# Adding the last quarter of each first product in PSUM, onto a copy that ScalarE makes

## The chip, the cores and the metric

The kernel runs on one core of a Trainium2 chip. The metric is the device time of one launch in microseconds (us), as a median over runs. Five engines work side by side, each through its own queue in program order: TensorE (PE, matrix products; its weight loads are shown apart as PEld), VectorE (DVE), ScalarE (ACT), GpSimd (POOL) and SyncE (SP, which issues most DMAs).

## The reference, cut to what matters

```python
# attention: B, H, S, D = 4, 8, 768, 64, in blocks of 64 tokens, with a decay lam per head
for b in range(nb):
    intra = einsum('bhij,bhjd->bhid', einsum('bhic,bhjc->bhij', qb, kb) * Dmask, vb)
    inter = einsum('bhid,bhde->bhie', qb * lam_pow, kv_state)
    out[:, :, sl] = intra + inter
    kv_state = lam_block * kv_state + einsum('bhsd,bhse->bhde', kb * rev_pow, vb)
x = out.transpose(0, 2, 1, 3).reshape(3072, 512)
# four experts (branches), all of them for every token
p = domain_probs / (domain_probs.sum(-1, keepdims=True) + 1e-09)
for e in range(4):
    h = np.maximum(x @ w1[e], 0.0)           # 3072x512 @ 512x1024
    out += p[:, e:e + 1] * (h @ w2[e])       # 3072x1024 @ 1024x512
```

All is float32. The two products with w1 and w2 are nearly all of the arithmetic.

## The kernel before, in words

The 3072 tokens go in three groups of 1024, and a *unit* is one expert on one group: twelve units, numbered 0 to 11. For each unit the *first product* is relu(x @ w1) and the *second product* is the gated product with w2. While unit `at` has its second product, unit `at + 1` has its first one: TensorE goes back and forth between the two. Attention of the later groups is put between them in the first units.

Both products use Strassen's scheme in Winograd's form: seven products M1 to M7 in place of eight, with sums before and after. The first product uses it twice, so one unit's first product consists of seven outer products `m` (in the order `SEQ` = M1, M5, M6, M2, M7, M3, M4), and each of those has seven inner ones `i` (in the order `INNER` = M1, M7, M6, M4, M5, M2, M3). An outer product is called a *product* below, and an inner one a *piece*. One piece is two fp32 matmuls of 128x128 by 128x256 into the two halves of one PSUM bank; the profile shows each matmul as two records, so a piece is four.

`first_product` (matmuls at L1053) works with two PSUM banks, g1 and g3. Pieces are summed in PSUM as far as Winograd's sums allow, and the bank is read in between:

- g1: M1 begins; it is read for quarter "11"; M6 is added, read for "21"; M5 is added, read for "22"; M3 is added, read for "12".
- g3: M7 begins, read for "22"; M4 is added, read for "21"; then a fresh bank is begun by M2, read for "11".

A read is an addition by VectorE (`tt`, L117) into the quarter's SBUF tile `new[at]`, 128x512, or a copy by ScalarE (L1061) where nothing is there yet to add to. The next matmul that writes the same bank has to wait for the read. Products that finish one quarter of relu(x @ w1) (`OUT` = M2, M3, M4) are passed through a relu by ScalarE in place (L1065). From unit 5 on (`NEST` = 5) the gate is multiplied in at once, by GpSimd in place (`gated`, L117 on POOL), because these units have a nested second product. `finished` and `later` add M5's, M6's and M7's sums afterwards as background steps; there ScalarE copies one operand into a PSUM bank (`bring`, "up" at L985, 128x512 from SBUF to PSUM) and VectorE adds from it.

The second product has two forms. In units 0 to 4 it is *flat* (`second_product`, L1107): each of its seven steps has four parts of four matmuls, eight records each. In units 5 to 11 it is *nested* (`nested_product`, L1406): each step has seven pieces b0 to b6, of two matmuls, four records, each; VectorE adds each to `sums` after it is made.

So there are 77 first products beside a second one: 35 beside a flat one (of units 1 to 5) and 42 beside a nested one (of units 6 to 11). The order of TensorE's work within each pair is written out by hand, in eight *slots* x = 0 to 7. `a` is the list of the first product's pieces and `b` that of the second product's:

```python
elif nested:
    order = [b[0:2], a[0:2], b[2:4], a[2:4], b[4:6], a[4:6], b[6:8], a[6:8]]
else:
    order = [b[0:1], a[0:2], b[1:2], a[2:4], b[2:3], a[4:6], b[3:5], a[6:8]]
```

The last entry of `a` is `finished`, and b[7] (nested) or b[4] (flat) is a step that issues nothing on TensorE. Between the slots a background step may be taken (`rest`, `take`): sums for later operands (`hT`, `xs`, `sums<-sums,jp`) on VectorE, with their copies by ScalarE (`hp` at L905). Weights and other work for GpSimd are let out by counters (`pump`, `fits`) that the planner keeps of each engine's supposed load.

Of the kernel before, what the change touches and what calls it, by code (L numbers as in the profile page):

```python
# [11 lines left out]
AF = mybir.ActivationFunctionType  # L12
ALU = mybir.AluOpType
# [8 lines left out]
def kernel(  # L22
# [30 lines left out]
    nc = tc.nc  # L53

    B, H, S, D = q.shape
    E, DM, F = moe_w1.shape
    NTOK, DOUT = out.shape
    P = nc.NUM_PARTITIONS
# [9 lines left out]
    W = 512  # L68
# [20 lines left out]
    def bank(tag, name):  # L89
        return ps.tile([P, W], FP32, name=name, tag=tag)  # L90
# [25 lines left out]
    def tt(eng, o, a, b, op):  # L116
        eng.tensor_tensor(out=o, in0=a, in1=b, op=op)  # L117
        if eng is nc.gpsimd:
            busy[0] = max(busy[0], now[0]) + math.prod(o.shape[1:]) / (640 if spare else 480)
        else:  # L120
            vector(math.prod(o.shape[1:]), PSUM in (a.space, b.space))

    def vector(n, psum):
        filled[0] = max(filled[0], now[0] + psum / 2) + 0.09 + n * (0.31 if psum else 0.8 if spare else 0.49) / 512
# [14 lines left out]
    unit_of = {u: x for x, u in enumerate(units)}  # L139
    NEST = 2 * E - 3  # L140
# [52 lines left out]
    def store(f):  # L193
        queue.append((busy[0] + (8 if spare else 2), f))
# [35 lines left out]
    def inner(eng, what, to, blk, ops, at):  # L230

        b = {n: blk[:, i, j * 256:(j + 1) * 256] for n, (i, j) in at.items()}
        s = stage.tile([P, 4, 256], FP32, name="ops", tag="st")
        for i, (name, x, y, op) in enumerate(ops):
            b[name] = s[:, SLOT[name]]
            tt(eng, b[name], b[x], b[y], op)
        pieces = [(to[:, 1:5], s[:])]
        if A_OF[what[2]][0] == "S":
            pieces += [(to[:, 0], blk[:, 0, 0:256]), (to[:, 5:7], blk[:, 1].rearrange("p (a f) -> p a f", a=2))]
        store(lambda: ([send(out=x, in_=y) for x, y in pieces], made.add(what)))  # L240
# [81 lines left out]
    INNER = ("M1", "M7", "M6", "M4", "M5", "M2", "M3")  # L322
# [194 lines left out]
    for r in range(2):  # L517
        for ac in range(NHP):
            h = 4 * r + ac
            nc.vector.tensor_tensor_scan(  # L520
                out=s_decay[:, r, ac], data0=lam_bc[:, h:h + 1].to_broadcast([P, BL]), data1=blk_ident,
# [10 lines left out]
    for ac in range(NHP):  # L532
        nc.vector.tensor_tensor_scan(
            out=q_decay[:, ac], data0=lam_q[:, ac:ac + 1].to_broadcast([P, BL]), data1=zeros[:, 0:BL],
# [22 lines left out]
    gate_bc = decay[:]  # L557
# [40 lines left out]
    def after(slots, f):  # L598

        f = functools.partial(f)  # L600
        f.at = now[0] + slots
        return f
# [10 lines left out]
    def rest(n=1, force=False):  # L613
        for _ in range(n):
            take(background, force)
# [262 lines left out]
    outer = {e: {n: {} for n in ("B11", "B12", "B21", "B22", "T1", "T2", "T3", "T4")} for e in range(NEST, len(units))}  # L878
    within = {}

    def gated(e, i, j, at, t):

        def step():
            n = j * 4 + (int(at[1]) - 1) * 2
            x = t[:].rearrange("p (c t) -> p c t", c=2)
            by = gate_bc[:, n:n + 2].rearrange("p n t -> p (n t)").unsqueeze(1).to_broadcast([P, 2, 256])
            tt(nc.gpsimd, x, x, by, ALU.mult)
            outer[e][f"B{i + 1}{j + 1}"][at] = t

        aside.append(after(2, step))  # L890
# [84 lines left out]
    OUT = {"M2": (0, 0), "M3": (0, 1), "M4": (1, 0)}  # L975

    def finished(g, e, m, blocks, new):

        def later(to, a, b, order, relu=False):
            there = dict(a)  # L980

            def bring(at):

                there[at] = bank("s" + "01"[order.index(at) % 2], "up")
                nc.scalar.copy(out=there[at][:], in_=a[at][:])  # L985

            def step(at):
                x = there[at]
                if unit_of[g, e] >= NEST and at != order[-1]:
                    bring(order[order.index(at) + 1])  # L990
                o = to[at] if at in to else small("m" + at)
                tt(nc.vector, o[:], x[:], b[at][:], ALU.add)
                if relu:
                    nc.scalar.activation(out=o[:], in_=o[:], func=AF.Relu)
                    if unit_of[g, e] >= NEST:
                        gated(unit_of[g, e], 1, 1, at, o)
                to[at] = o
                blocks["left"] -= 1

            blocks["left"] = 4  # L1000
            if unit_of[g, e] >= NEST:
                background.append(lambda: bring(order[0]))
            background.extend(lambda at=at: step(at) for at in order)

        def keep(c, i, j):
            if unit_of[g, e] >= NEST:
                outer_sums(unit_of[g, e], *{(0, 1): (("T1",), ("T3", "T2")), (1, 0): (("T4",),)}.get((i, j), ()))
                return
            hid[g, e, i, j] = {"A11": c["11"], "A12": c["21"], "A22": c["22"], "A21": c["12"]}
            operands((g, e, i, j))  # L1010

        if m == "M6":
            blocks["U2"], blocks["U4"] = new, {}
            later(blocks["U4"], new, blocks["M5"], ("11", "22", "21", "12"))
        elif m == "M7":
            blocks["U3"] = new
            later(blocks["M5"], new, blocks["M5"], ("11", "12", "21", "22"), relu=True)
            keep(blocks["M5"], 1, 1)
        elif m in OUT:
            keep(new, *OUT[m])  # L1020
        else:
            blocks[m] = new

    def settle(m, blocks):

        while m in ("M7", "M4") and blocks["left"]:
            rest(force=True)

    def first_product(g, e, m, blocks, tags):

        while (g, e, m) not in fed:
            pump(force=True)
        while unit_of[g, e] in (1, 2 * E) and to_do.get(m):
            take(own_sums, True)
        until(("x", g, m))
        ws, t = fed.pop((g, e, m)), slots[m]
        xs = {i: t[:, X_AT[i]] for i in X_AT}
        settle(m, blocks)
        old = {
            "M1": None, "M5": None, "M6": blocks.get("M1"), "M2": blocks.get("M1"), "M7": blocks.get("U2"),  # L1040
            "M3": blocks.get("U4"), "M4": blocks.get("U3"),
        }[m]
        new = {n: small("m" + n) for n in ("11", "12", "21", "22")} if m in ("M1", "M5", "M6") else old
        banks = {}

        def inner(i):
            t = tags[0] if i in ("M1", "M6", "M5", "M3") else tags[1]
            fresh = i in ("M1", "M7", "M2")
            if fresh:
                banks[t] = bank(t, "p" + t)  # L1050
            p = banks[t]
            for j in range(2):
                nc.tensor.matmul(  # L1053
                    out=p[:, j * 256:(j + 1) * 256], lhsT=ws[i][:, j * P:(j + 1) * P], rhs=xs[i],
                    start=(fresh and j == 0), stop=True, skip_group_check=True,
                )
            at, begins = READ[i]
            if not begins:
                tt(nc.vector, new[at][:], p[:], new[at][:], ALU.add)
            elif old is None:  # L1060
                nc.scalar.copy(out=new[at][:], in_=p[:])  # L1061
            else:
                tt(nc.vector, new[at][:], p[:], old[at][:], ALU.add)
            if m in OUT and (at == "12" or not begins):
                nc.scalar.activation(out=new[at][:], in_=new[at][:], func=AF.Relu)  # L1065
                if unit_of[g, e] >= NEST:
                    gated(unit_of[g, e], *OUT[m], at, new[at])

        return [lambda i=i: inner(i) for i in INNER] + [lambda: finished(g, e, m, blocks, new)]


    acc = {}
# [477 lines left out]
    blocks = {}  # L1550
# [114 lines left out]
    for at, (g, e) in enumerate(units):  # L1665
# [14 lines left out]
        blocks, banks = {}, {}  # L1680
        for i in range(7):
# [8 lines left out]
            if nests and i == 2:  # L1690
                nc.scalar.dma_start(
                    out=gate_bc, in_=gate_rows[ahead[0] - 1, :, ahead[1]].partition_broadcast(P),
                )
            if nested:
                pair = (at * 7 + i) % 2 if ahead else i % 3
                b = nested_product(at, SEQ3[i], (("q01", "q02"), ("q11", "q12"), ("g1", "g3"))[pair])
                if i < 6 and (at, SEQ3[i + 1]) != PLAIN:
                    inner_sums(at, SEQ3[i + 1])
            else:
                b = second_product(g, e, SEQ2[i], banks)  # L1700
# [4 lines left out]
            a = []  # L1705
            if ahead:
                a = first_product(*ahead, SEQ[i], blocks, ("g1", "g3"))
# [3 lines left out]
            if not ahead:  # L1711
                order = [[], b[0:2], [], b[2:4], [], b[4:6], [], b[6:]]
            elif nested:
                order = [b[0:2], a[0:2], b[2:4], a[2:4], b[4:6], a[4:6], b[6:8], a[6:8]]
            else:
                order = [b[0:1], a[0:2], b[1:2], a[2:4], b[2:3], a[4:6], b[3:5], a[6:8]]
            turned_back = list(after_last.get(SEQ3[i], ())) if nested and not ahead else []
            if at == i == 0:
                for m in SEQ[1:]:
# [74 lines left out]
```

## Time and profile before

| what | value |
|---|---|
| median of 3 runs | 1158.81 us (1156.0 to 1160.66) |
| profiled execution: time, span of its instructions | 1160.19 us, 1158.4 us |
| granted TensorE clock | 0.999 |
| busy: PE, PEld | 1144.7 us (99%), 991.0 us (86%) |
| busy: DVE, ACT, POOL | 833.0 us (72%), 317.4 us (27%), 795.2 us (69%) |
| matmuls of the first products (L1053) with streamed weights | 1960 records, 472.5 us busy |
| VectorE's additions out of g1 and g3 (`m<-pg,m`) | 451, 687 ns each |
| ScalarE's copies out of g1 and g3 (L1061) | 88, 586 ns each |
| ScalarE's relus in place (L1065) | 132, 630 ns each |

A record of TensorE's that the profile gives 0.38 us begins 0.216 us after the one before it when nothing is waited for: records overlap. So PE looks busy nearly everywhere, and a stall must be read from where the next record starts and from the idle time of PEld. "m" is any SBUF tile of a quarter, "pg" the banks g1 and g3, "pq" the banks of the nested second product.

### The profile page before, as it was taken

How to read it: one execution, taken by the hardware profiler on the slowest of the kernel's cores; microseconds unless marked ns; L12 is line 12 of the kernel's file. 1: busy time of each engine (PE TensorE's matmuls, PEld its weight loads, DVE VectorE, ACT ScalarE, POOL GpSimd, SP SyncE). 2: the span in 40 equal slices, each digit the busy share in tenths (PEclk: the TensorE clock that was granted, in tenths of full speed). 3: DMA queues.
4: the chain of work that ended last, by engine and by line, in shares of the span. 5: the costliest groups of instructions: out<-in, count | busy, mean ns of one | idle time of the engine just before them, and what ended most of it. 6: DMA issues, size and time to landing. Idle time of an engine off the chain costs nothing.

```text
span 1158.4 us, 22016 instructions
## 1 busy us (share of the span) xinstructions
PE 1144.7 (99%) x8011; PEld 991.0 (86%) x8011; DVE 833.0 (72%) x1484; ACT 317.4 (27%) x645; POOL 795.2 (69%) x752
## 2 busy tenths in 40 slices
PE   8999999999999999999999999999999999999998
PEld 7888888888888888888888888888888888888887
DVE  4677885588488757946775667999876667777785
ACT  3322122112201211221243342232343341341232
POOL 2738318647742975774794998996896883893894
PEclk9999999999999999999999999999999999999999
DMA  8886667999899899896867659976678857566542
GB/s 192 179 274 191 172 194 222 293 283 291 269 318 309 261 302 300 273 344 201 277 204 237 191 162 298 308 245 207 207 234 260 230 178 215 170 189 193 158 191 73
DMA packets 309259, 269.21 MB, mean 232 GB/s; under 512 B 141536, under 2 KB 244128, under 8 KB 309152
## 3 DMA queue, kind: packets, MB, share of 16 engines
q1 hardware_dynamic: 290832, 262.53, 74.3%
q10 hardware_dynamic: 18320, 5.28, 2.1%
q8 instruction: 64, 1.05, 0.4%
q14 instruction: 43, 0.35, 0.1%
HBM read 194.83 MB, written 77.10 MB: 235 GB/s over the span
## 4 chain that ended last, share of the span: by engine, by line
PE 86%; DVE 6%; DMA 3%; SPq 2%; POOL 1%; issue 1%; ACT 0%; ACTq 0%; DVEq 0%; POOLq 0%
PE pg L1053 36%; PE pq L1406 22%; PE q L1107 17%; DVE m L117 2%; PE pM L1508 2%; PE pc L1508 2%; SPq L114 2%; DVE sums L117 1%; PE sp L700 1%; PE op L754 1%; DMA w_ops<-w1o 1%; PE op L772 1%; PE sp L707 1%; DVE xs L117 1%; PE qp L670 1%
## 5 line engine op out<-in xcount | busy, mean ns | idle before, releaser
L1053 PE MATMUL pg<-xs,ws_in 128*128 128x256 f32 x1960 | 472.5, 381 | 3.2 <-DVE m L117 3.1
L1053 PEld LDWEIGHTS pg<-xs,ws_in 128*128 128x128 f32 x1960 | 368.7, 190 | 58.4 <-DVE m L117 8.4
L117 DVE TENSOR_TENSOR m<-pg,m 128x512 f32<-128x512 f32 x451 | 307.0, 687 | 111.6 <-PE pg L1053 98.1
L1107 PE MATMUL q<-w2t,m 128*128 128x256 f32 x1120 | 265.8, 380 | 0.5 <-DVE m L117 0.5
L1107 PEld LDWEIGHTS q<-w2t,m 128*128 128x128 f32 x1120 | 211.9, 190 | 30.2 <-DVE m L117 1.2
L117 POOL TENSOR_TENSOR m<-m,decay 128x512 f32<-128x512 f32 x112 | 141.6, 1287 | 80.8 <-ACT m L1065 72.9
L1406 PE MATMUL pq<-acc,w2t 128*128 128x256 f32 x688 | 169.5, 379 | 0.2 <-DVE sums L117 0.2
L117 DVE TENSOR_TENSOR sums<-pq,sums 128x256 f32<-128x256 f32 x272 | 112.9, 420 | 67.7 <-PE pq L1406 58.8
L1406 PEld LDWEIGHTS pq<-acc,w2t 128*128 128x128 f32 x688 | 130.3, 190 | 18.9 <-issue 0.5
L1065 ACT ACTIVATE m<-m 128x512 f32<-128x512 f32 x132 | 82.9, 630 | 197.0 <-DVE m L117 179.1
L117 DVE TENSOR_TENSOR m<-m,m 128x512 f32<-128x512 f32 x112 | 101.2, 904 | 3.5 <-ACT m L1065 3.5
L1125 DVE SCALAR_TENSOR_TENSOR acc<-q,gate,acc 128x256 f32<-128x256 f32 x108 | 51.9, 481 | 59.3 <-PE q L1107 58.9
L1061 ACT COPY m<-pg 128x512 f32<-128x512 f32 x88 | 51.6, 586 | 146.8 <-PE pg L1053 139.8
L117 POOL TENSOR_TENSOR acc<-hT,hT 128x512 f32<-128x512 f32 x56 | 70.5, 1275 | 12.5 <-PE pq L1406 12.5
L117 POOL TENSOR_TENSOR acc<-hT,acc 128x512 f32<-128x512 f32 x56 | 71.4, 1275 | 6.5 <-PE pq L1406 1.8
L1406 PE MATMUL pq<-hT,w2t 128*128 128x256 f32 x288 | 74.0, 379 | 0.1
L117 POOL TENSOR_TENSOR w2o<-w2b 128x512 f32<-128x512 f32 x26 | 33.8, 1319 | 50.1 <-DMA w2b<-in_moe_w_dram 42.7
L985 ACT COPY up<-m 128x512 f32<-128x512 f32 x56 | 32.5, 588 | 126.8 <-DVE m L117 116.1
L1406 PEld LDWEIGHTS pq<-hT,w2t 128*128 128x128 f32 x288 | 54.6, 190 | 7.9 <-DVE sums L117 0.5
L905 ACT COPY hp<-m 128x512 f32<-128x512 f32 x84 | 48.4, 589 | 40.2 <-DVE hT L117 21.5
L1406 PE MATMUL pq<-m,w2t 128*128 128x256 f32 x228 | 58.5, 380 | 0.1
L117 POOL TENSOR_TENSOR xs<-xs 128x256 f32<-128x256 f32 x28 | 24.4, 872 | 44.8 <-DMA xs<-x_blocks 43.2
(141 smaller groups left out, 1368.4 us busy)
## 6 DMA issues: line engine op xcount, KB each, us to landing
w2t<-w_ops SPq DMA_DIRECT2D x129, 256.0 KB, 3.0
ws_in<-w_ops SPq DMA_DIRECT2D x40, 512.0 KB, 4.8
ws_in<-w_ops SPq DMA_DIRECT2D x60, 256.0 KB, 4.0
ws_in<-w_ops SPq DMA_DIRECT2D x40, 384.0 KB, 4.1
w2b<-in_moe_w_dram SPq DMA_DIRECT2D x56, 256.0 KB, 5.4
w_ops<-ops SPq DMA_DIRECT2D x28, 512.0 KB, 4.6
w2t<-w_sums SPq DMA_DIRECT2D x40, 256.0 KB, 4.5
w_sums<-w2o SPq DMA_DIRECT2D x16, 512.0 KB, 5.1
```

The lines of the kernel that those rows point to most:

```text
L114: (by or nc.sync).dma_start(out=out, in_=in_)
L117: eng.tensor_tensor(out=o, in0=a, in1=b, op=op)
L670: nc.tensor.transpose(out=x[:, ac * C:(ac + 1) * C], in_=y[:, 2 * ac:2 * ac + 2].rearrange("p r d -> p (r d)"), identity=ident[:],)
L905: nc.scalar.copy(out=there[x][:], in_=blk[at][:])
L985: nc.scalar.copy(out=there[at][:], in_=a[at][:])
L1053: nc.tensor.matmul(out=p[:, j * 256:(j + 1) * 256], lhsT=ws[i][:, j * P:(j + 1) * P], rhs=xs[i], start=(fresh and j == 0), stop=True, skip ...
L1061: nc.scalar.copy(out=new[at][:], in_=p[:])
L1065: nc.scalar.activation(out=new[at][:], in_=new[at][:], func=AF.Relu)
L1107: nc.tensor.matmul(out=p[:, s * DH:(s + 1) * DH], lhsT=h[A_OF[m]][:, c * 256 + s * P:c * 256 + (s + 1) * P], rhs=fed2[g, e, m][uu][:, c], ...
L1125: nc.vector.scalar_tensor_tensor(out=o, in0=x, scalar=w, in1=o, op0=ALU.mult, op1=ALU.add)
L1406: nc.tensor.matmul(out=p[:, 0:256], lhsT=fed3[e, m, x // 2][:, x % 2, c * P:(c + 1) * P], rhs=b[B_OF[i]][:, c * 256:(c + 1) * 256], start= ...
L1508: nc.tensor.matmul(out=p[:, s * 256:(s + 1) * 256], lhsT=a[c][:, f:f + P], rhs=b[:, c, j * 256:(j + 1) * 256], start=(s == 0 and c == 0 an ...
```

## The change

The order of the pieces becomes `FIRST`: M1, M7, M6, M4, M5, nothing, M3, M2. M5 is alone in slot 5, and M2 comes last, after M3, in slot 7. M2 no longer begins a fresh, empty bank. When M5 has been issued, ScalarE copies quarter "11" (M1's part, with what it was added to) from SBUF into a fresh bank g3 (`seed`), and M2 is added onto that by TensorE. What M2 leaves in the bank is then the finished quarter, and one instruction reads it (`last`): a ScalarE copy (44 products), a ScalarE relu (12, in units 1 to 4), or from unit 5 on one VectorE instruction that does the relu and the gate at once (21). VectorE's addition for "11", its relu by ScalarE and, from unit 5 on, its gate by GpSimd go. In `finished` the background sums take the quarters in the order 22, 21, 11, 12, where quarter "11" came first before.

```diff
+    def by_gate(j, at):
+        n = j * 4 + (int(at[1]) - 1) * 2
+        return gate_bc[:, n:n + 2].rearrange("p n t -> p (n t)").unsqueeze(1).to_broadcast([P, 2, 256])
+
...
-            later(blocks["U4"], new, blocks["M5"], ("11", "22", "21", "12"))
+            later(blocks["U4"], new, blocks["M5"], ("22", "21", "11", "12"))
...
-            later(blocks["M5"], new, blocks["M5"], ("11", "12", "21", "22"), relu=True)
+            later(blocks["M5"], new, blocks["M5"], ("22", "21", "11", "12"), relu=True)
...
+    FIRST = ("M1", "M7", "M6", "M4", "M5", None, "M3", "M2")
 
     def first_product(g, e, m, blocks, tags):
...
+        def seed():
+            banks[tags[1]] = bank(tags[1], "p" + tags[1])
+            nc.scalar.copy(out=banks[tags[1]][:], in_=new["11"][:])
+
+        def last(p, o):
+            if m not in OUT:
+                nc.scalar.copy(out=o[:], in_=p[:])
+            elif unit_of[g, e] < NEST:
+                nc.scalar.activation(out=o[:], in_=p[:], func=AF.Relu)
+            else:
+                i, j = OUT[m]
+                vector(W, True)
+                nc.vector.scalar_tensor_tensor(
+                    out=o[:].rearrange("p (c t) -> p c t", c=2), in0=p[:].rearrange("p (c t) -> p c t", c=2), scalar=0.0,
+                    in1=by_gate(j, "11"), op0=ALU.max, op1=ALU.mult,
+                )
+                outer[unit_of[g, e]][f"B{i + 1}{j + 1}"]["11"] = o
+
         def inner(i):
             t = tags[0] if i in ("M1", "M6", "M5", "M3") else tags[1]
-            fresh = i in ("M1", "M7", "M2")
+            fresh = i in ("M1", "M7")
...
+            if i == "M2":
+                last(p, new["11"])
+                return
+            if i == "M5":
+                seed()
...
-        return [lambda i=i: inner(i) for i in INNER] + [lambda: finished(g, e, m, blocks, new)]
+        return [i and (lambda i=i: inner(i)) for i in FIRST] + [lambda: finished(g, e, m, blocks, new)]
...
-                order = [b[0:2], a[0:2], b[2:4], a[2:4], b[4:6], a[4:6], b[6:8], a[6:8]]
+                order = [b[0:2], a[0:2], b[2:4], a[2:4], b[4:6], a[4:6], b[6:8], a[6:]]
             else:
-                order = [b[0:1], a[0:2], b[1:2], a[2:4], b[2:3], a[4:6], b[3:5], a[6:8]]
+                order = [b[0:1], a[0:2], b[1:2], a[2:4], b[2:3], a[4:6], b[3:5], a[6:]]
```

More of the change, by code (lines that the diff above doesn't have):

```diff
@@ L879 @@
     within = {}
+    def by_gate(j, at):
+        n = j * 4 + (int(at[1]) - 1) * 2
+        return gate_bc[:, n:n + 2].rearrange("p n t -> p (n t)").unsqueeze(1).to_broadcast([P, 2, 256])
     def gated(e, i, j, at, t):
         def step():
-            n = j * 4 + (int(at[1]) - 1) * 2
             x = t[:].rearrange("p (c t) -> p c t", c=2)
-            by = gate_bc[:, n:n + 2].rearrange("p n t -> p (n t)").unsqueeze(1).to_broadcast([P, 2, 256])
-            tt(nc.gpsimd, x, x, by, ALU.mult)
+            tt(nc.gpsimd, x, x, by_gate(j, at), ALU.mult)
             outer[e][f"B{i + 1}{j + 1}"][at] = t
```

## The prediction

> **What bounds the kernel now.** I read the page first: engine shares, the chain that ended last, and the groups of the first product.
>
> ```profile
> PE 1144.7 (99%) x8011; PEld 991.0 (86%) x8011; DVE 833.0 (72%) x1484; ACT 317.4 (27%) x645; POOL 795.2 (69%) x752
> ...
> PE 86%; DVE 6%; DMA 3%; SPq 2%; POOL 1%; issue 1%; ACT 0%; ACTq 0%; DVEq 0%; POOLq 0%
> ...
> L1053 PEld LDWEIGHTS pg<-xs,ws_in 128*128 128x128 f32 x1960 | 368.7, 190 | 58.4 <-DVE m L117 8.4
> L117 DVE TENSOR_TENSOR m<-pg,m 128x512 f32<-128x512 f32 x451 | 307.0, 687 | 111.6 <-PE pg L1053 98.1
> L1107 PE MATMUL q<-w2t,m 128*128 128x256 f32 x1120 | 265.8, 380 | 0.5 <-DVE m L117 0.5
> ```
>
> TensorE is the bound: 99% busy, 86% of the chain, and the chain names hardly anything else that the change touches. VectorE, ScalarE and GpSimd have room on the average. So work taken off them is worth only the stalls of TensorE that it ends, and work put on them costs only the stalls that it makes. The waits of PEld tell how much there is to gain:
>
> ```profile
> PEld pg L1053 <- DVE m L117: 8.4, 17, 1.4
> ...
> PEld q L1107 <- DVE m L117: 1.2, 2, 0.9
> PEld pq L1406 <- DVE sums L117: 1.1, 3, 0.5
> ```
>
> These are microseconds in total, times, longest. Were all waits of the two products on VectorE to go, 8.4 + 1.2 + 1.1 = 10.7 us would be the most, 0.9%.
>
> Then I read one nested product slot by slot, in the timeline (start, us, engine):
>
> ```profile
> 639.32 1.89 PE L1053 MATMUL pg<-xs,ws_in 128*128 128x256 f32 x8
> ...
> 640.38 0.69 DVE L117 TENSOR_TENSOR m<-pg,m 128x512 f32<-128x512 f32 x1 [0.44 <-PE pg L1053]
> ...
> 641.05 1.03 PE L1406 MATMUL pq<-hT,w2t 128*128 128x256 f32 x4
> ...
> 641.25 0.69 DVE L117 TENSOR_TENSOR m<-pg,m 128x512 f32<-128x512 f32 x1 [0.17 <-PE pg L1053]
> 641.70 0.84 PEld L1053 LDWEIGHTS pg<-xs,ws_in 128*128 128x128 f32 x4
> 641.91 1.03 PE L1053 MATMUL pg<-xs,ws_in 128*128 128x256 f32 x4
> ```
>
> The first row is M5 and M2 (eight records, 8 x 0.216 = 1.73 us), then comes b6 (four, 0.864 us), then M3. M3 writes the bank that M5 wrote, so it must wait for VectorE's read of M5, the row at 640.38. That one begins 0.416 us after M5's last record started (639.32 + 3 x 0.216 = 639.97) and ends at 641.07. M3's weight load is not due before 641.70: 0.6 us to spare, because M2 and b6 lie between. The other short distances in this bank are M3 to the next product's M1 (b0 and b1 between, 1.73 us), and M1 to M6 and M6 to M5 (2.59 us).
>
> What a late read costs is seen where M3 did wait:
>
> ```profile
> 713.90 1.28 DVE L117 TENSOR_TENSOR m<-pg,m 128x512 f32<-128x512 f32 x2
> ...
> 714.63 0.73 PEld L1053 LDWEIGHTS pg<-xs,ws_in 128*128 128x128 f32 x4 [0.38 <-DVE m L117]
> 714.64 1.13 PE L1053 MATMUL pg<-xs,ws_in 128*128 128x256 f32 x4
> ```
>
> M5's read is the first of the two, over at 714.58. The load starts 0.04 us after it (43 ns wherever I looked), and the four records take 1.13 in place of 1.03 us: the first holds TensorE for 0.320 in place of 0.216 us, as the weight load, normally 0.21 us ahead and hidden, is now in the way. So a read that ends at time t lets the matmul work as if begun at t + 0.043 + 0.104 = t + 0.147 us.
>
> **The change, part by part.** TensorE: the same 8011 records, in another order; 0 us of work.
>
> VectorE loses 77 additions, 77 x 0.687 = 52.9 us, and gains 21 instructions of relu and gate. No row has that form; a row of the kind with 256 elements takes 481 ns (L1125) against 420 for an addition of that size (L117, `sums<-pq`), so between 0.687 + 0.061 and 0.687 + 0.122; I take 0.75, 21 x 0.75 = 15.8 us. Net -37 us. GpSimd loses 21 x 1.287 = 27 us. ScalarE gains 77 seeds at 0.588 (the `up` copies, L985, same shape and direction) = 45.3, 44 copies at 0.586 = 25.8, 12 relus out of PSUM at 0.6 = 7.2, and loses 33 x 0.630 = 20.8: net +57 us, to 32% of the span. All of it lies beside TensorE.
>
> Distances in the banks, which is what counts:
>
> - M3 to the next M1: M2 now lies between too, 1.73 becomes 2.59 us. The stalls there shrink: 0.94 and 0.37 us in nested products, 1.2 in a flat one.
> - The seed waits for VectorE's read of M4 and is needed at M2: M5, b6 and M3 lie between, 2.59 us, for a 0.59 us copy. In the trace M4 is read by 1.14 us after its last record (median), that is before M5 begins. Hidden, with some 1.8 us to spare; it would cost if ScalarE were held longer than that at that moment. Queued behind a seed on ScalarE are the `hp`/`up` copies and relus, which nobody on TensorE waits for within 2 us.
> - M2's reader is waited for by the next M7: b0, b1 and M1 between, 2.59 us for a read that takes 0.42 + 0.59 to 0.75. Hidden.
> - **M5 to M3: M2 is gone from between.** Beside a flat product b3 stays, eight records, 1.73 us. Beside a nested one only b6 is left, 0.864 us.
>
> For nested products, then: M3 is due 4 x 0.216 + 0.216 = 1.080 us after M5's last record starts. The read ends 1.107 us after it at the least (0.416 + 0.692), and nothing in the change makes it earlier: VectorE cannot start before M5 is done. I took the end of this read from the timeline for each of the 42 nested products. 19 end at 1.107 to 1.110, 16 at 1.172 to 1.174 (a background sum is just ahead of them), and seven are late: 1.573, 1.792, 2.026, 2.094, 2.239, 2.241 and 2.412 us. In the program's order after the change, the same VectorE instructions stand ahead of M5's read in all but one of the 42.
>
> - 19 x (1.108 + 0.147 - 1.080) = 19 x 0.175 = 3.3 us
> - 16 x (1.173 + 0.147 - 1.080) = 16 x 0.240 = 3.8 us
> - seven late ones: 14.38 + 7 x (0.147 - 1.080) = 7.85 us. From this goes what VectorE's backlog costs there today: five stalls at M3 (1.57 + 5 x 0.104 = 2.1 us), three of the second product right behind them (0.224, 0.226, 0.320 and some 0.1 each, 1.1 us) and two at M1 (0.94 + 0.37 + 0.2 = 1.5 us, of which I count half, because VectorE is busy without a gap there and the delay shows up again at the next M5). Net 7.85 - 2.1 - 1.1 - 0.75 = 3.9 us.
>
> Flat products: three reads of M5 are later than 1.73 us of cover allows, +1.3 us; against it two stalls behind VectorE's backlog (1.2 at 387 us and 0.7 at 582 us, 2.1 us with the resume) shrink by the removed addition's 0.69 us each, -1.4. Net 0.
>
> Sum: 3.3 + 3.8 + 3.9 + 0 = +11.0 us. On the profiled execution's 1160.19 that is 1171.2; the median of the runs is 1.4 us lower, so I say 1170.
>
> [...] The trace shows the load itself waiting (714.63) and 0.104 us paid for it. [...] The wait stands on the load here, so I go by the row.
>
> [...]
>
> **The rivals.**
>
> *Faster.* VectorE's relief ends the stalls and M5 to M3 costs nothing. It decides at a read that ends within 1.080 - 0.147 = 0.93 us; no read of the 42 is under 1.107. Its price would be at most -10.7 us, more likely -6: about 1153. Chance 0.04.
>
> *The same.* The stall is there, but resumes without the 0.104 us, and the late seven are wholly made up by VectorE's relief: 35 stalls of 0.07 to 0.14, 7.2 - 3.6 = 3.6 us, 1162.5. For it: VectorE loses four of seven additions per unit, 2.7 us of the some 85 that a unit takes. Against: the backlogs build up within one product, out of `xs` and `hT` sums that stay. Chance 0.11.
>
> *Slower still, by ScalarE.* A seed that comes late stops M2. `hp` copies wait for GpSimd's gate (18.7 us in five waits, the longest 5.8), with the seed queued behind. Today the last of these ends 0.8 us before M5 starts, 3 us before the seed must be done; it decides if that moves by over 2 us. One or two such waits in each of six units at 1 us: +9, 1179. Chance 0.08.
>
> *Forecast.* Slower by the M5 to M3 stall, 1166 to 1176. Chance 0.77.
>
> **How the numbers follow.** A measurement of this kernel can tell about 0.5% from no change, 5.8 us, so slower begins at 1164.6. The forecast's ends come from the late seven counted at 0 and without any deduction (7.1 and 15 us); with the rivals at both sides the range is 1163 to 1178. Slower 0.77 + 0.08 = 0.85, same 0.11, faster 0.04.
>
> **What would show it.** Right: PEld's wait on DVE m for pg grows from 17 times and 8.4 us to some 45 times and about 20 us, nearly all at M3 in nested products, 0.1 to 0.2 us longer each than the read's lag; VectorE's busy time falls by 37 us, ScalarE's rises by 57, and the span grows all the same. Wrong: M3 starting on time beside b6, or PE waiting for ACT at M2 in many products.

## The result, and the profile after

The changed kernel takes 1167.33 us (median of 4 runs, 1166.07 to 1168.09) against 1158.89 us, now over four runs: the ratio is 1.0074, with a 95% interval of 1.0052 to 1.0097. It is slower by 8.4 us. The profiled execution took 1168.09 us, with a span of 1166.3, 7.9 us more than the one shown before.

First the page: engines, and the groups that answer to those of before (idle time of the engine after the bar, with what ended it).

```profile
PE 1150.8 (99%) x8011; PEld 989.0 (85%) x8011; DVE 787.6 (68%) x1428; ACT 369.8 (32%) x745; POOL 771.4 (66%) x731
...
L1075 PEld LDWEIGHTS pg<-xs,ws_in 128*128 128x128 f32 x1960 | 366.5, 190 | 69.0 <-DVE m L117 20.2
L117 DVE TENSOR_TENSOR m<-pg,m 128x512 f32<-128x512 f32 x374 | 255.7, 687 | 111.2 <-PE pg L1075 99.2
...
L1052 ACT COPY pg<-m 128x512 f32<-128x512 f32 x77 | 45.4, 590 | 134.2 <-DVE m L117 127.1
...
L1062 DVE SCALAR_TENSOR_TENSOR m<-pg,decay 128x512 f32<-128x512 f32 x21 | 14.4, 687 | 2.8 <-PE pg L1075 2.6 <-DMA w_ops<-ops 0.2
```

The L1052 row is the seeds, the L1062 row the 21 instructions of relu and gate. VectorE has 45 us less to do and GpSimd 24 us less, and ScalarE 52 us more, as the change says. TensorE executes the same 8011 records. What grew is the time in which weight loads of the first product wait for VectorE's reads. The waits of PEld (us in total, times, longest) answer to the rows of before:

```profile
PEld pg L1075 <- DVE m L117: 20.2, 44, 1.4
...
PEld pq L1433 <- DVE sums L117: 1.6, 4, 0.6
...
PEld q L1134 <- DVE m L117: 1.1, 2, 0.9
...
PEld pg L1075 <- ACT m L1058: 0.4, 1, 0.4
```

17 waits of 8.4 us have become 44 of 20.2; the prediction's sign of being right was some 45 and about 20. The last row is the one wait of the first product for ScalarE in that list, and it is for a relu's read of the bank (`last`), not for a seed. Here is the same nested product as before, by the timeline:

```profile
638.10 0.58 ACT L1052 COPY pg<-m 128x512 f32<-128x512 f32 x1
...
638.29 1.03 PE L1075 MATMUL pg<-xs,ws_in 128*128 128x256 f32 x4
...
639.16 1.03 PE L1433 MATMUL pq<-hT,w2t 128*128 128x256 f32 x4
639.36 0.69 DVE L117 TENSOR_TENSOR m<-pg,m 128x512 f32<-128x512 f32 x1 [0.44 <-PE pg L1075]
...
640.10 0.94 PEld L1075 LDWEIGHTS pg<-xs,ws_in 128*128 128x128 f32 x5 [0.32 <-DVE m L117]
640.11 1.13 PE L1075 MATMUL pg<-xs,ws_in 128*128 128x256 f32 x4
```

The seed (first row) starts before M5 (638.29) does and is over at 638.68; M2 comes over two microseconds later. M5's read ends at 640.05. M3 would have begun at 640.02 (b6 began at 639.16, plus 0.864), with its load at 639.81; the load starts at 640.10 instead, and the four records take 1.13 in place of 1.03 us. That is 0.09 + 0.10 = 0.19 us lost, in a product in which nothing else was late.

Read off the starts of all records, M3 is late in all 42 nested products and, beside flat ones, in one. The table gives those nested stalls for each kernel (lateness of the first record, plus the up to 0.104 us by which it holds the next; only stalls over 0.1 us are counted), beside the times. "Cover" is the time of the matmuls that lie between M5 and M3.

| kernel | cover M5 to M3, nested | M3 late, of 42 | sum, us | median time, us | ratio to before (95%) |
|---|---|---|---|---|---|
| before | 1.73 us | 5 | 2.1 | 1158.89 | 1 |
| the change | 0.86 us | 42 | 13.4 | 1167.33 | 1.0074 (1.0052 to 1.0097) |
| order alone, no seed | 0.86 us | 42 | 12.7 | 1169.54 | 1.0087 (1.0063 to 1.0110) |
| M2 ahead of M3 | 1.73 us | 3 | 0.9 | 1157.03 | 0.9974 (0.9961 to 0.9986) |
| no cover | 0 | 42 | 45.9 | 1214.43 | 1.0473 (1.0450 to 1.0495) |
| beside flat alone | 1.73 us (as before) | 5 | 2.0 | 1158.61 | 0.9997 (0.9985 to 1.0008) |
| b5 between | 1.73 us | 9 | 4.7 | 1158.20 | 0.9992 (0.9981 to 1.0004) |
| slots as before, with seed | 1.73 us | 4 | 1.7 | 1157.44 | 0.9982 (0.9970 to 0.9994) |
| seed twice | 0.86 us | 42 | 13.3 | 1170.24 | 1.0090 (1.0069 to 1.0111) |
| both moves | 2.59 us | 0 | 0 | 1153.88 | 0.9947 (0.9935 to 0.9958) |
| beside nested alone | 0.86 us | 42 | 13.3 | 1171.44 | 1.0095 (1.0080 to 1.0109) |

### The profile page after: what moved, and what is told of

It is laid out like the page before. It is cut to its first block, busy times and chain, and to the rows that moved or that the text cites. A ratio compares the mean times of both kernels' runs of the same rounds, so it can differ in the third digit from the quotient of the medians.

```text
span 1166.3 us, 22155 instructions
## 1 busy us (share of the span) xinstructions
PE 1150.8 (99%) x8011; PEld 989.0 (85%) x8011; DVE 787.6 (68%) x1428; ACT 369.8 (32%) x745; POOL 771.4 (66%) x731
## 3 DMA queue, kind: packets, MB, share of 16 engines
q8 instruction: 64, 1.05, 0.4%
## 4 chain that ended last, share of the span: by engine, by line
PE 92%; DVE 5%; issue 1%; DMA 1%; ACT 0%; SPq 0%; ACTq 0%; DVEq 0%
PE pg L1075 39%; PE pq L1433 21%; PE q L1134 20%; PE pM L1535 3%; DVE m L117 2%; PE pc L1535 2%; DVE sums L117 2%; PE sp L700 1%; PE op L754 1%; PE op L772 1%; PE sp L707 1%; DVE xs L117 1%; PE qp L670 1%; PE kp L670 1%; DMA y<-parked 1%
## 5 line engine op out<-in xcount | busy, mean ns | idle before, releaser
L1075 PEld LDWEIGHTS pg<-xs,ws_in 128*128 128x128 f32 x1960 | 366.5, 190 | 69.0 <-DVE m L117 20.2
L117 DVE TENSOR_TENSOR m<-pg,m 128x512 f32<-128x512 f32 x374 | 255.7, 687 | 111.2 <-PE pg L1075 99.2
L117 POOL TENSOR_TENSOR m<-m,decay 128x512 f32<-128x512 f32 x91 | 115.3, 1280 | 97.9 <-ACT m L1092 83.5
L1092 ACT ACTIVATE m<-m 128x512 f32<-128x512 f32 x99 | 62.4, 630 | 194.7 <-DVE m L117 192.7
L1088 ACT COPY m<-pg 128x512 f32<-128x512 f32 x88 | 51.6, 586 | 127.0 <-PE pg L1075 120.6
L1052 ACT COPY pg<-m 128x512 f32<-128x512 f32 x77 | 45.4, 590 | 134.2 <-DVE m L117 127.1
L1056 ACT COPY m<-pg 128x512 f32<-128x512 f32 x44 | 25.8, 586 | 87.5 <-PE pg L1075 84.3
```

The costliest lines, as they stand in the source:

```text
L1052: nc.scalar.copy(out=banks[tags[1]][:], in_=new["11"][:])
L1056: nc.scalar.copy(out=o[:], in_=p[:])
L1075: nc.tensor.matmul(out=p[:, j * 256:(j + 1) * 256], lhsT=ws[i][:, j * P:(j + 1) * P], rhs=xs[i], start=(fresh and j == 0), stop=True, skip ...
```

## The experiments

The theory is that of the prediction: what costs is the distance from M5 to M3. The rival is the seed: ScalarE's copy, and M2's wait for it.

**The order without the seed.** The kernel before, with the change's order and slots; M2 begins an empty bank and VectorE adds it.

```diff
+    FIRST = ("M1", "M7", "M6", "M4", "M5", None, "M3", "M2")
...
-        return [lambda i=i: inner(i) for i in INNER] + [lambda: finished(g, e, m, blocks, new)]
+        return [i and (lambda i=i: inner(i)) for i in FIRST] + [lambda: finished(g, e, m, blocks, new)]
...
-                order = [..., a[4:6], b[6:8], a[6:8]]
+                order = [..., a[4:6], b[6:8], a[6:]]
...
-                order = [..., a[4:6], b[3:5], a[6:8]]
+                order = [..., a[4:6], b[3:5], a[6:]]
```

> The order M1, M7, M6, M4, M5, nothing, M3, M2 in the kernel before, with no seed: M2 begins an empty bank and VectorE adds it, as before. If the short distance from M5 to M3 beside a nested second product is the cost, M3 stalls in all 42 nested products by 0.19 or 0.25 us and by more in the late ones, and the time is 1166 to 1170 us. If ScalarE's seed, and M2's wait for it, is the cost, nothing of it is left here and the time is 1159 us.

1169.54 us, as the distance theory said and within the interval of the change itself. M3 stalls in all 42 nested products, 0.19 or 0.25 us each where nothing is late. Without a single seed, the whole loss is there. In the same product:

```profile
639.90 1.03 PE L1055 MATMUL pg<-xs,ws_in 128*128 128x256 f32 x4
...
640.96 0.69 DVE L117 TENSOR_TENSOR m<-pg,m 128x512 f32<-128x512 f32 x1 [0.44 <-PE pg L1055]
...
641.71 0.30 PEld L1055 LDWEIGHTS pg<-xs,ws_in 128*128 128x128 f32 x2 [0.32 <-DVE m L117]
```

The idle 0.32 us ahead of M3's weight load is the same as in the change. The background sums keep their old order here, quarter "11" first, while the runs below that lose nothing have the change's order of them: that part of the change is not the cause either.

**M2 ahead of M3.** The change with its last two pieces swapped.

```diff
-    FIRST = ("M1", "M7", "M6", "M4", "M5", None, "M3", "M2")
+    FIRST = ("M1", "M7", "M6", "M4", "M5", None, "M2", "M3")
```

> The change with its last two pieces swapped: M5, nothing, M2, M3. Between M5 and M3 there are 1.73 us again, and M2 comes 0.86 us earlier behind the seed. By the distance theory the 42 stalls go, only a few late ones stay, and with the lighter VectorE the time is 1155 to 1159 us. By the seed theory M2 has less time to wait for the seed and the time is 1167 us or more.

1157.03 us. All seeds, and the lighter VectorE, are kept; 39 of the 42 stalls are gone, and the kernel is faster than before by 0.14 to 0.39%. One M2 waited, by 0.39 us. The waits of PEld on the first product's reads (44 times, 20.2 us in the change):

```profile
PEld pg L1075 <- DVE m L117: 3.4, 7, 1.1
```

**No cover.** b6 goes ahead of M5, so that M3 follows M5 at once.

```diff
-                order = [b[0:2], a[0:2], b[2:4], a[2:4], b[4:6], a[4:6], b[6:8], a[6:]]
+                order = [b[0:2], a[0:2], b[2:4], a[2:4], b[4:8], a[4:6], [], a[6:]]
```

> The change with b6 moved ahead of M5 in nested products, so that M3 follows M5 at once. By the distance theory each of the 42 stalls grows by b6's 0.864 us, to some 1.05 and 1.12 us: 42 x 0.864 = 36 us more than the change, 1199 to 1205 us. By the seed theory nothing depends on b6's place but the time for the seed, which is 0.86 us shorter: 1167 to 1175 us.

1214.43 us: 47 us more than the change, where 36 were expected, and 9 us over the upper end. At M3 it went as expected: the typical stall is 1.05 us, and the sum rose from 13.4 to 45.9, by 32.5 us. The rest is in the second product, whose late starts rose from 2.8 to 18.0 us. The timeline shows both:

```profile
666.33 0.68 DVE L117 TENSOR_TENSOR m<-up,m 128x512 f32<-128x512 f32 x1
...
666.93 0.75 DVE L117 TENSOR_TENSOR sums<-pq,sums 128x256 f32<-128x256 f32 x2
667.39 0.73 PEld L1433 LDWEIGHTS pq<-m,w2t 128*128 128x128 f32 x4 [0.91 <-DVE sums L117]
667.39 1.13 PE L1433 MATMUL pq<-m,w2t 128*128 128x256 f32 x4 [0.50 <-DVE sums L117]
...
668.36 1.03 PE L1075 MATMUL pg<-xs,ws_in 128*128 128x256 f32 x4
...
669.43 0.69 DVE L117 TENSOR_TENSOR m<-pg,m 128x512 f32<-128x512 f32 x1 [1.75 <-PE pg L1075]
...
670.17 1.13 PE L1075 MATMUL pg<-xs,ws_in 128*128 128x256 f32 x4 [0.78 <-DVE m L117]
```

b6 (667.39) writes the bank that b4 wrote, and now has only b5 between: the same kind of wait, in the other pair of banks, with VectorE late behind a background sum (the row at 666.33). M3 then begins 1.81 us after M5 (668.36 to 670.17) in place of 0.864.

**Beside flat products alone.** The whole change where the second product is flat, the old order of the pieces and no seed elsewhere. (The background sums keep the change's order in all units, here and in the last run.)

```diff
+        seeded = unit_of[g, e] <= NEST
-            fresh = i in ("M1", "M7")
+            fresh = i in (("M1", "M7") if seeded else ("M1", "M7", "M2"))
-            if i == "M2":
+            if seeded and i == "M2":
-            if i == "M5":
+            if seeded and i == "M5":
-        return [i and (lambda i=i: inner(i)) for i in FIRST] + ...
+        return [i and (lambda i=i: inner(i)) for i in (FIRST if seeded else INNER)] + ...
```

> The whole change, seed and order, in the 35 products beside a flat second product alone; the 42 nested ones stay as before. By the distance theory a flat product keeps 1.73 us between M5 and M3 and loses nothing: 1157 to 1159 us. By the seed theory 35 of 77 seeds cost their share of 8.4 us: 1162 to 1164 us.

1158.61 us, ratio 0.9997: 35 seeds cost nothing, and with 1.73 us of cover left the new order costs nothing either.

**b5 between.** b5 goes behind M5, M2 stays last.

```diff
-                order = [b[0:2], a[0:2], b[2:4], a[2:4], b[4:6], a[4:6], b[6:8], a[6:]]
+                order = [b[0:2], a[0:2], b[2:4], a[2:4], b[4:5], a[4:6], b[5:8], a[6:]]
```

> The change with one piece moved in nested products: b5 goes from before M5 to after it, so that b5 and b6 (1.73 us) lie between M5 and M3; M6 to M5 shrinks from 2.59 to 1.73 us in turn, and M2 stays last behind the seed. By the distance theory the 42 stalls go as they did with M2 ahead of M3, now with 2.59 us left from M3 to the next M1: 1155 to 1158 us. If it were M2's late place or its seed that costs, nothing would change: 1167 us.

1158.20 us, just over the upper end: the loss is cured, but nothing is gained. Nine late M3 remain, 4.7 us, and two M5, which now have 1.73 us behind M6, wait 0.7 us together.

```profile
PEld pg L1075 <- DVE m L117: 9.6, 17, 1.3
```

Where VectorE is free M3 is on time; where it works through a backlog, moving M5 ahead of b5 brings M5 forward by 0.864 us and its read by less. In the unit with the longest waits (M1's and M5's products) the read ended 2.24 us after the start of M5's last record before, and 2.76 and 2.77 us here: it came forward by some 0.34 us. In two products whose read was on time before, it even came 0.3 to 0.4 us later, counted from M4's start (4.35 us before, 4.64 and 4.71 here).

**Slots as before, with the seed.** M5 and M2 in slot 5, M3 in slot 7, the seed right behind M4's read.

```diff
-    FIRST = ("M1", "M7", "M6", "M4", "M5", None, "M3", "M2")
+    FIRST = ("M1", "M7", "M6", "M4", "M5", "M2", "M3")
-            if i == "M5":
-                seed()
             if not begins:
                 tt(nc.vector, new[at][:], p[:], new[at][:], ALU.add)
+                if i == "M4":
+                    seed()
```

> Seed and accumulation in PSUM in the slots of the kernel before: M5 and M2 in slot 5, M3 in slot 7, the seed issued right behind M4's read. M5 to M3 is 1.73 us as before. By the distance theory there is no loss, and the lighter VectorE takes some of the old stalls: 1155 to 1159 us, less good than b5 between if M2 now waits for its seed, which has some 0.8 us to spare behind M4's read and none where that read is late. By the seed theory: over 1162 us.

1157.44 us. Two M2 waited for their seed (1.2 us together), fewer than feared; the kernel is faster than before by 0.06 to 0.3%. The seed, with the lighter VectorE and the other order of the background sums that come with it, is thus a small gain, and it was the order of the pieces that cost.

**Every seed twice.**

```diff
-            nc.scalar.copy(out=banks[tags[1]][:], in_=new["11"][:])
+            for _ in range(2):
+                nc.scalar.copy(out=banks[tags[1]][:], in_=new["11"][:])
```

> The change with every seed copied twice by ScalarE (77 x 0.59 = 45 us more of its time, M2 released 0.59 us later). By the distance theory the seed has over 1 us to spare at M2 and nothing changes: 1166 to 1169 us. If the seeds were what costs, doubling them would cost about as much again as the change did: 1175 us or more.

1170.24 us: 2.9 us over the change and 1.2 over what the distance theory allowed, far under what the seed theory asked for; the intervals of the two ratios overlap. No M2 waited, and the stalls at M3 are the same 13.3 us. Where the 2.9 us are, if they are real, is only partly seen: one stall of 1.1 us at an M5 and 0.9 us more in the nested second products. The M5 waited for VectorE's read of M6, which stood behind an `xs` sum that took 1.51 us, where the sum in this place took 0.64 us in the change. That is part of the delay; what lengthened the sum is not settled.

**Both moves.** b5 behind M5, and M2 ahead of M3.

```diff
-    FIRST = ("M1", "M7", "M6", "M4", "M5", None, "M3", "M2")
+    FIRST = ("M1", "M7", "M6", "M4", "M5", None, "M2", "M3")
-                order = [..., b[4:6], a[4:6], b[6:8], a[6:]]
+                order = [..., b[4:5], a[4:6], b[5:8], a[6:]]
```

> The change with both moves that cured the stall: b5 after M5, and M2 ahead of M3, beside nested products M5, b5, b6, M2, M3. M5 to M3 is 2.59 us, M3 to the next M1 and M6 to M5 are 1.73 us, M2 has 1.73 us and its own 0.21 us for the seed. If late reads of M5 are what is left at M3 in the two cures alone (4.7 us with b5 between, 0.9 us with M2 ahead of M3), they go: 1155 to 1157.5 us. If VectorE's backlog only moves to the next short distance (M6 to M5, M3 to M1), it is 1157 to 1159 us.

1153.88 us, ratio 0.9947 (0.9935 to 0.9958): faster than the kernel before and than the change, and better than both expectations, whose lower ends were 1155 and 1157 us. The waits of PEld on the first product's reads:

```profile
PEld pg L1075 <- DVE m L117: 2.2, 6, 0.7
```

Six waits of 2.2 us are left of 17 and 8.4 before. The late reads of M5 are as late as with b5 between (2.76 us), but M3 is due at 2.8 us. With 1.73 us at the other short reuses, little of the backlog comes out elsewhere: two M1 stall, 1.1 us together, and one M5 and one M2 lose 0.1 us each. How much of the gain this order would give without the seeds, no run shows.

**Beside nested products alone.** As beside flat alone, with `seeded = unit_of[g, e] > NEST`.

> The change beside nested second products alone, the 35 flat ones as before: the counterpart of the run beside flat ones, which gave no difference. By the distance theory all of the loss is here: 1166 to 1169 us. If the seeds cost by their number, 42 of 77, it is 1163.5 us.

1171.44 us, 2.4 us over the upper end. The 42 stalls at M3 are the same 13.3 us as in the change, and the flat products keep their old stalls (2.5 us at M1 and M3, against 0.9 in the change). So all of the loss is on this side. It is 4.1 us more than the change in the medians, but the two intervals of the ratios overlap. Of the 4.8 us between the two profiled spans, 1.4 are the flat products' old stalls (less an M7 of 0.3 us that only the change has), 1.1 are one M1 behind attention, which waited for a weight's DMA, 0.3 are in the second products, and 2.0 lie where the profiles differ from kernel to kernel (the matmuls that begin the kernel and attention's transposes, see below).

## Why the prediction was right, point by point

*The place.* M5 to M3 beside nested products was named as the cost, and it is: it appears with the order alone and no seed (12.7 us at M3, against 13.4 with the seeds), goes with either cure down to 0.9 and 4.7 us, and grows when b6 is taken away, by 32.5 us over the 42 products, where b6's time is 42 x 0.864 = 36.3.

*The quiet products.* 19 x 0.175 and 16 x 0.240 us were forecast. Measured: 0.186 to 0.189 and 0.248 to 0.257, some 0.012 us more each. The form of the price was right, but one figure in it was read too low: the weight load starts 0.053 us after the read's end and the matmul 0.055 us, in the five stalls of M3 before as in all 42 after, and not 0.043. (The rows shown say so too: 714.58 to 714.63.) So a read that ends at t lets the matmul work as if begun at t + 0.159 us, and the sum for 35 is 7.7 in place of 7.2 us.

*The seven late ones* were the mis-sized term. 7.85 us were forecast; the same seven products lost 0.40, 0.79, 0.68, 0.66, 0.65, 1.26 and 1.26 = 5.7 us. Three of the seven make up most of the difference, for two reasons that the trace shows. In two of them b6 itself began some 0.5 us late, waiting for VectorE, so that M3 was due later: the reads ended 2.10 and 2.09 us after M5 and cost 0.68 and 0.66 us, where the formula gives 1.16. In another, VectorE was less far behind: 1.32 in place of 2.03 us.

*The deductions.* The five old stalls at M3 (2.1 us) went into the new ones, as counted. The two at M1 (1.5 us) are gone altogether, where half was taken off. The three stalls of the second product, counted as gone (1.1 us), are gone, but others came in their place: the two late b6 just named, 0.5 us each, and one of 0.95 us in the last unit's second product, which has no first product beside it. All of them together are 2.5 us before and 2.8 us after. Nested products together: 13.4 - 2.1 - 1.5 + 0.3 = +10.1 us, against 11.0 forecast.

*Flat products.* Net 0 was forecast, from two terms of which neither came as sized. The late reads of M5 were to cost 1.3 us more; with the lighter VectorE the latest of them ended 1.98 us after M5's last record began in place of 3.30, and M3's stalls fell from 0.65 to 0.19 us. The two stalls behind VectorE's backlog were to shrink by 0.69 us each: the M1 at 387 us did, by 0.62, and the one of the second product at 582 us stayed, 0.8 us before and after. One M7 waited 0.28 us for ScalarE's relu of M2, a wait that the prediction had as hidden. The first product's stalls at M1, M3, M6 and M7 went from 2.1 to 1.2 us, -0.9. Another 2.0 us that came off, in the matmuls that begin the kernel (2.7 to 1.6 us) and in attention's transposes (2.0 to 1.1), were in no step. In the eleven profiles these two range from 0.8 to 2.9 and from 0.4 to 2.0 us, so I read them as scatter and not as the change's; each of these profiles is of another kernel, and no second profile of the same one shows it. 10.1 - 0.9 - 2.0 = +7.2 us, with 7.9 in the span; the sum of 11.0 was too high by the late products, M1's stalls, the flat products and the scatter, and too low by the 0.5 us of the quiet ones and the second product's new stalls. That the errors partly cancel is luck; that the loss sits at M3 is not.

*Work beside TensorE.* The relu and gate in one takes 687 ns, the same as the plain addition, and not 0.75 us. ScalarE's rise was forecast as 57 and is 52 us, GpSimd's fall as 27 and is 24. VectorE's fall was forecast as 37 and is 45: the additions out of the banks and their replacement make 36.9 (307.0 - 255.7 - 14.4), the `xs` sums take 5.9 us less, and the rest is in small groups. None of this was on the path, as said: VectorE and GpSimd lost 69 us of work together, and the span grew all the same.

*The weight loads.* The trace after bears out the row that the prediction went by: M3's load starts 0.053 us after the read's end and the four records take 1.13 us; no M3 of the 42 lost less than 0.186 us, 0.104 of it by this. None of the 42 loads started before the read had ended: the earliest came 0.052 us behind it, the latest 0.054.

*The rivals.* ScalarE made no M2 wait in the change. The faster case's condition, a read within 0.93 us, never held: the earliest ended at 1.107. Nor did that of the same time, a stall that resumes without the 0.104 us: all 42 paid it.

*The range.* Its two ends stand on different bases: 1166 is 7.1 us on the median of the runs, 1176 is 15 us on the profiled execution (1175.2). On the median alone they would have been 1166 and 1174; the measured 1167.33 lies in both.

## What to carry to other kernels

When pieces of work are put in another order, list for every buffer the time from its last write, through its reader, to its next write, and compare it with the reader's whole turnaround, here 1.11 us and 0.16 us to start again. Relief for an engine that is not the bound is worth at most the stalls that it causes (by the waits before, 10.7 us here), and brought less in these runs (0.14 to 0.39% of the time with M2 ahead of M3); one reuse distance that falls short by 0.2 us in 35 products, and by more in seven others, cost 13.4 us. Where a distance is short, spread the pieces evenly over both lists of work before taking anything away: the kernel with these seeds, 8 us slower than before in this order, is 6 us faster than before with M5, b5, b6, M2, M3.

## What the runs showed that I had not expected

The reads that TensorE waited for were late for two different reasons, and the runs that cured the one did not all cure the other. Where VectorE was free, 1.73 us of cover was enough: 37 of 42 M3 were on time before, 39 with M2 ahead of M3, 33 with b5 between. Where it had a backlog, bringing the write forward by 0.864 us brought the read forward by less (0.34 us) or not at all: with the same 1.73 us of cover, b5 between left 4.7 us and M2 ahead of M3 0.9 us.

A relu, a multiplication and a read out of PSUM in one VectorE instruction cost the same 687 ns for 128x512 (21 instructions) as one addition (374), though the smaller form with a per-partition scalar takes 481 against 420 ns for 128x256.
